# Batch 0 of a two-part attention and feed-forward kernel: pair 1's query copy on VectorE, sink rows loaded instead of copied, and another order of 390 pieces

## The chip, the cores and the metric

The kernel runs on one core of a Trainium2 chip. Its time is the device time in microseconds (us) of one execution; several runs are taken and their median is compared. Five engines work side by side, each through its own list of instructions in order: TensorE (PE in the profile, PEld for its weight loads), VectorE (DVE), ScalarE (ACT), GpSimd (POOL) and SyncE (SP), which here only issues loads and stores. Sixteen DMA engines move the data that SP, POOL and ACT ask for. PE writes to PSUM, a memory of eight banks, and the other engines bring results from there to SBUF. An instruction that needs another engine's result waits for a semaphore, and everything behind it on its engine waits with it.

## The reference

Attention over 4 batches, 8 heads, 768 tokens and 64 dimensions per head, and then a feed-forward layer with leaky slopes on all 3072 tokens:

```python
rel = pos[:, None] - pos[None, :]
causal = rel >= 0
stream_keep = causal & ((pos[None, :] < n_sink) | (rel < window))      # n_sink 4, window 64
mask = causal if is_retrieval[h] else stream_keep                       # heads 0, 2, 6 are retrieval heads
scores = where(mask, q @ k.T / sqrt(64), -1e9)
x = softmax(scores) @ v            # heads side by side: [3072, 512]
h = x @ w_in                       # [3072, 2048]
g = max(h, 0) + alpha * min(h, 0)
out = g @ w_out                    # [3072, 512]
```

A retrieval head sees all earlier tokens. A streaming head sees the last 64 tokens and the first four, the sink tokens.

## The kernel before

The heads of a batch are taken in four pairs, (2, 6), (1, 5), (0, 4), (3, 7). A pair of one batch has a number n from 0 to 15, so batch 0 has pairs 0 to 3. Pair 0 has two retrieval heads, pairs 1 and 3 two streaming heads, and pair 2 one of each (head 4 streams). The attention output of a batch becomes `xT`, and the feed-forward layer then works in token tiles t (512 and 256 tokens of each batch) and blocks f of 128 of the 2048 hidden features.

Every step is a small function with a name, and one list, `ORDER` (L14 to L81), says in which order the 1215 pieces are issued. Since each engine goes through its own instructions in that order, the list is the schedule of all engines at once. The names that matter here, with n the pair and hh the head within it:

- `Lq`, `Lk`, `Lv`: loads of queries, keys and values as 32-bit rows (SP's queue, L234 to L282); `Cq`, `Ck`, `Cv`: casts to bf16, in batch 0 mostly on POOL (L347 to L392).
- `Tq`, `Tk`: transposes of queries and keys by PE into a PSUM bank (L398); `tq`, `tk`: copies from there to SBUF (L408, L416). `tq` is on ACT but for `tq0.1`; `tk` is on VectorE in batch 0.
- `S`: scores on PE, into one of two double banks in batch 0; `s`: their exponential on ACT; `A`: scores times values on PE; `a`: the division on VectorE; `X`, `x`: transpose into `xT` on PE and its copy on VectorE.
- `wi`, `wo`: loads of the feed-forward weights, issued by POOL; `P`, `p`, `g`: first product, ReLU on ACT and slope on VectorE; `O`, `Q`: second product.
- `warm0` to `warm8`: 32, 3, 14 and then 4 each of dummy matmuls on PE (70 are used, `warm1` is not), and `kz`, `qz`, `vz`, `sz`, `so`, `ro`: fills.

In batch 0 a streaming head's keys are cut into seven tiles of 128 rows, four of which are the sink rows, repeated at the head of each tile. For the values, tile i holds rows 124 i to 124 i + 127, so its first four rows are at first ordinary rows of the sequence. `load_rows` (L261) loads tiles 0 to 5 of a head with one DMA of 128 partitions x 6 runs of 256 B (L277) and the short seventh tile with another one of 24 partitions (L282). The cast brings all to `vb`, and then `sinks` (L337) copies the four rows of tile 0 over the first four rows of tiles 1 to 6: on POOL for pairs 1 and 2 and head 3, on VectorE for head 7 (L387, L392).

On POOL the pieces of batch 0 come in this order: casts of keys and queries of pairs 1 to 3, the value cast `Cv0`, weights `wi1a wi0a wi1b wi0b`, `Cq3`, `Cv1`, `Cv2`, weights `wi6 wi7 wi5`, `Cv3.0`, `wi4`, `Cq4`, `Ck4.0`, `wi2`, `wi3`, `Ck4.1`, `Cq5`, and weights `wo`. On SP: `Lq0 Lk1 Lq1 Lk0 Lk2 Lq2 Lv0 Lk3 Lv1 Lq3 Lv2 Lv3 Lq4 Lk4 Lq5 Lk6 Lq6 Lk5` and on.

Of the kernel before, what the change touches and what calls it, by code (L numbers as in the profile page):

```python
# [17 lines left out]
Lk3 S0.1.0 kfz0 Lv1 vo ro0 Ck3.1 s0.1.0 Lq3 Ck3.0 wi1a wi0a wi1b wi0b Cq3 sz0 idf S1.0.0 so2 Al s1.0.0 so0 al S0.1.1  # L18
s0.1.1 Lv2 Tq2 Tk2 tk2.1 tk2.0 S0.1.2 S1.0.1 A0.0 s0.1.2 a0.0 Cv1 A0.1 a0.1 Cv2 s1.0.1 tq2 S1.1.1 Tk3 S2.0.1 tk3.0
s1.1.1 S2.0.2 X0 s2.0.1 x0 wi6 s2.0.2 wi7 Lv3 Lq4 Tq3 tk3.1 S2.0.0 wi5 m4.0.2 warm6 S2.1.0 A1.0 a1.0 Lk4 tq3 A1.1  # L20
Cv3.0 s2.0.0 Lq5 Lk6 Lq6 Lk5 wi4 Cq4 a1.1 S3.0.0 s2.1.0 A2.0 s3.0.0 X1 x1 S3.0.1 S3.1.1 Ck4.0 P0.2.0 s3.0.1 A3.0 a2.0
Lq7 a3.0 S2.1.1 s3.1.1 wi2 s2.1.1 Cv3.1 S3.1.0 wi3 A2.1 Ck4.1 Cq5 wo1 s3.1.0 P0.1.0 P0.3.0 A3.1 Lk7 P0.0.0 Tq4 a2.1
tq4 X2 a3.1 X3 Lv5 Tk4 x2 P0.2.1 Lv6 P0.1.1 tk4.0 P0.3.1 P0.0.1 x3 Tq5 tq5 tk4.1 P0.0.2 P0.1.2 wo0 p0.0 P0.3.2 P0.13
p0.13 g0.0 P0.14 g0.13 P1.14 wo3 p0.1 p1.14 g0.1 P1.2 p1.2 P0.8 Lv4 g1.14 Ck6.0 P0.9 g1.2 Cq6 m8.0.2 p0.8 nr p0.9 g0.8
m12.1.2 p0.3 near0 near2 P0.15 S4.0.5 p0.14 P1.10 s4.0.5 Ck6.1 P0.11 P0.2.2 g0.9 Ck5.1 g0.14 p0.15 p1.10 P1.0 Lq8 Tq6
ro1 Ck5.0 g0.15 p0.2 g0.3 S4.1.0 g1.10 wo2 p0.11 P1.12 P1.8 P0.7 g0.2 Lk8 s4.1.0 kfz1 g0.11 Lk9 p1.0 P0.5.0 p1.12 tq6
g1.0 P0.5.1 Tk5 P0.4.0 p1.8 P0.6 tk5.0 g1.8 p0.7 P0.4.1 g1.12 P0.5.2 P0.4.2 p0.6 tk5.1 P0.10 g0.7 p0.4 p0.10 g0.6
S4.0.3 s4.0.3 S4.0.0 P1.4 g0.4 Tk6 g0.10 S4.0.1 S5.1.0 m4.0.3 P1.6 p0.5 tk6.1 Ck7.0 near1 D1.0 P0.12 tk6.0 O0.0.0 g0.5
O0.0.1 p1.6 Lv7 p0.12 g1.6 p1.4 S6.1.1 D1.1 s5.1.0 s4.0.0 S5.1.1 S4.1.2 g1.4 m4.1.0 s4.0.1 s4.1.2 Z1.0.1 s6.1.1 s5.1.1
# [36 lines left out]
s14.0.4 m14.1.2 S14.0.1 b3.4.0 P5.0 a13.1 b4.4.0 p5.0 Q4.0.3 s14.0.1 Q4.0.7 g5.14 S15.1.2 g5.0 S14.1.1 S14.0.5 S15.0.0  # L66
m13.0.1 b5.4.0 m12.1.1 Z4.1.2 S14.0.0 b7.4.1 S15.1.1 m14.0.4 Q4.0.4 s15.1.2 Z4.1.4 s14.0.0 s14.1.1 s14.0.5 m14.0.0
m14.0.1 Cv14 m12.1.0 Q4.1.6 b6.4.0 s15.1.1 m14.0.5 A13.0 b2.4.1 m14.0.3 s15.0.0 S15.0.2 S15.1.0 S15.0.1 S14.1.0
s15.0.2 s14.1.0 m15.0.0 Q4.1.5 s15.1.0 m14.1.1 m14.1.0 A12.1 a13.0 A14.0 s15.0.1 m15.0.2 m15.1.1 a12.1 A14.1 a14.0
Q5.0.1 m15.1.0 a14.1 b3.4.1 b4.4.1 m15.0.1 Q4.1.7 m15.1.2 b1.5.0 X13 X12 b5.4.1 Q5.0.2 Q4.1.3 A15.0 Z5.0.1 X14 a15.0  # L70
A15.1 a15.1 Q4.1.4 b6.4.1 P6.8.0 X15 x15 P6.15.0 P6.4.0 b8.4.0 P6.8.1 P6.11.0 P6.10.0 b8.4.1 b7.5.0 P6.13.0 P6.4.1
# [5 lines left out]
Q6.0.6 b2.6.0 b1.6.1 P7.8 p7.12 Z6.1.3 Q6.0.5 p7.10 Q6.0.2 g7.10 Q6.1.2 g7.14 Z6.1.2 p7.8 g7.8 Q7.0.1 b3.6.0 b4.6.0
Q6.1.6 Z6.0.4 Q6.0.3 g7.12 b7.6.0 b8.6.0 b2.6.1 Q6.0.7 Z7.0.1 Z7.0.3 b3.6.1 b5.6.0 Q6.1.5 Q7.0.5 b4.6.1 Q6.0.4 Z6.1.4
b1.7.0 Z7.0.2 Q7.0.2 Q6.1.7 Q7.0.6 Q6.1.3 b5.6.1 b4.7.0 b2.7.0 b7.6.1 b7.7.0 b6.6.0 b8.6.1 b3.7.0 Q6.1.4 Q7.0.7 b6.6.1
Z7.0.4 Q7.0.3 b5.7.0 Q7.0.4 b8.7.0 b6.7.0  # L80
# [916 lines left out]
```

## Time and profile before

| | us |
|---|---|
| median of three runs | 222.54 (222.44 to 223.9) |
| span of the profiled execution, first to last instruction | 220.4 |
| PE busy in that span | 214.5 |
| VectorE busy | 188.0 |
| ACT busy | 145.8 |
| POOL busy | 45.6 |

The page gives the span of the profiled execution but no time of its own for it, so sums are made in the span, and what lies around it is the difference to the median, 2.1 us. A row of a timeline reads: start in us, duration in us, engine, source line of the kernel, operation, tile written <- tile read, shapes, count, and in brackets how long the engine was idle before and what ended that. A duration of several instructions in a row is one merged stretch. A "q" behind an engine is its queue of issues, so SPq L277 is SP issuing the DMA of line 277; how long that takes is not how long the data take. In a row of stretches stand the window, its length, the busy time of PE, PEld, VectorE, ACT and POOL with counts, the granted clock of PE, the share of time in which the 16 DMA engines were busy, and GB/s. In the part on DMA queues q1 holds the loads and stores that SP and ACT issue, q0 those of POOL: packets, MB and share of the 16 engines' span.

### The profile page before, as it was taken

How to read it: one execution, taken by the hardware profiler on the slowest of the kernel's cores; microseconds unless marked ns; L12 is line 12 of the kernel's file. 1: busy time of each engine (PE TensorE's matmuls, PEld its weight loads, DVE VectorE, ACT ScalarE, POOL GpSimd, SP SyncE). 2: the span in 40 equal slices, each digit the busy share in tenths (PEclk: the TensorE clock that was granted, in tenths of full speed). 3: DMA queues.
4: the chain of work that ended last, by engine and by line, in shares of the span. 5: the costliest groups of instructions: out<-in, count | busy, mean ns of one | idle time of the engine just before them, and what ended most of it. 6: DMA issues, size and time to landing. Idle time of an engine off the chain costs nothing.

```text
span 220.4 us, 5779 instructions
## 1 busy us (share of the span) xinstructions
PE 214.5 (97%) x2210; PEld 158.0 (72%) x2210; DVE 188.0 (85%) x471; ACT 145.8 (66%) x314; POOL 45.6 (21%) x92
## 2 busy tenths in 40 slices
PE   8989999999999999999999999999999999999993
PEld 7879866765465865577899666757889645888882
DVE  6879849979989897999998998999999767997841
ACT  4789659989999795657953165799783066816230
POOL 6679980620031200000004110100000200001000
PEclk9999999999999999999999999999999999999999
DMA  6999999999999999979999998791004310002124
GB/s 187 319 233 222 307 241 231 227 201 218 205 245 167 259 162 222 198 182 193 211 215 174 228 184 194 176 187 42 4 1 123 103 79 0 0 3 95 51 93 147
DMA packets 89655, 35.98 MB, mean 163 GB/s; under 512 B 76676, under 2 KB 87964, under 8 KB 89628
## 3 DMA queue, kind: packets, MB, share of 16 engines
q1 hardware_dynamic: 83484, 26.35, 59.4%
q0 software_dynamic: 5824, 8.93, 17.8%
q8 instruction: 17, 0.28, 0.5%
q10 hardware_dynamic: 320, 0.34, 0.5%
q14 instruction: 10, 0.08, 0.1%
HBM read 27.58 MB, written 6.29 MB: 154 GB/s over the span
## 4 chain that ended last, share of the span: by engine, by line
PE 92%; DVE 3%; ACT 2%; issue 1%
PE P L640 36%; PE P L718 28%; PE P L595 7%; PE P L660 7%; PE P L473 4%; PE P L814 3%; PE P L456 2%; PE P L406 2%; PE P L466 1%; PE P L620 1%; DVE kT L435 1%; PE P L544 1%; DVE g L652 1%; ACT neg L645 1%; ACT kT L435 0%
## 5 line engine op out<-in xcount | busy, mean ns | idle before, releaser
L640 PE MATMUL P<-xT,w_in_b 128*128 128x512 bf16 (+1 forms) x512 | 89.6, 326 | 0.0
L652 DVE SCALAR_TENSOR_TENSOR g<-neg,oma,P 128x256 bf16<-128x256 f32 (+1 forms) x128 | 71.7, 607 | 11.4 <-ACT neg L645 11.0
L645 ACT ACTIVATE neg<-P 128x512 f32<-128x512 f32 x96 | 55.4, 602 | 30.3 <-PE P L640 15.7
L640 PEld LDWEIGHTS <-w_in_b 128*128 128x128 bf16 x512 | 49.2, 98 | 29.1 <-issue 0.3
L718 PEld LDWEIGHTS <-g 128*128 128x128 bf16 x480 | 45.7, 98 | 8.1 <-issue 0.8
L512 ACT ACTIVATE eR<-P 128x448 bf16<-128x448 f32 (+4 forms) x63 | 37.0, 627 | 4.8 <-PE P L505 2.2
L718 PE MATMUL P<-w_out_b,g 128*128 128x256 bf16 x320 | 39.0, 273 | 0.0
L736 POOL DMA_DIRECT2D out_dram<-ot x14 | 7.6, 545 | 115.6 <-ACT ot L760 37.9
L560 ACT ACTIVATE eS<-P 128x352 bf16<-128x352 f32 x45 | 20.8, 494 | 2.3 <-PE P L473 1.4
L606 DVE TENSOR_TENSOR xn<-P,rcp 128x448 bf16<-128x448 f32 (+1 forms) x32 | 19.4, 607 | 1.1
L571 DVE TENSOR_TENSOR eS<-eS,ms_near 128x352 bf16<-128x352 bf16 x45 | 15.8, 363 | 0.7 <-ACT eS L560 0.6
L660 PE MATMUL P<-w_out_b,g 128*128 128x512 bf16 x64 | 15.8, 379 | 0.2 <-ACT kT L429 0.2
L703 DVE TENSOR_TENSOR g<-g 128x1024 bf16<-128x1024 bf16 x20 | 13.7, 683 | 0.1
L456 PE MATMUL P<-qT,kT 128*128 128x192 bf16 (+14 forms) x68 | 11.1, 251 | 0.2 <-ACT eS L566 0.2
L595 PEld LDWEIGHTS <-eS 128*128 128x128 bf16 x260 | 10.0, 97 | 1.3
L595 PE MATMUL P<-vb,eS 128*128 128x65 bf16 x260 | 10.8, 193 | 0.0
L522 DVE TENSOR_TENSOR eR<-eR,mr_near 128x128 bf16<-128x128 bf16 (+5 forms) x54 | 10.6, 223 | 0.0
L473 PE MATMUL P<-qT,kT 64*128 64x176 bf16 (+10 forms) x164 | 10.4, 249 | 0.0
L718 PE MATMUL P<-w,g 128*128 128x256 bf16 x80 | 10.4, 273 | 0.0
L660 PEld LDWEIGHTS <-g 128*128 128x128 bf16 x64 | 5.6, 97 | 6.3 <-issue 1.1
L595 PE MATMUL P<-vb,eR 128*128 128x65 bf16 x276 | 10.0, 193 | 0.0
L595 PEld LDWEIGHTS <-eR 128*128 128x128 bf16 x276 | 9.4, 97 | 0.6 <-issue 0.2
(130 smaller groups left out, 267.8 us busy)
## 6 DMA issues: line engine op xcount, KB each, us to landing
out_dram<-ot POOLq DMA_DIRECT2D x18, 256.0 KB, 3.2
rows<-in_k_dram SPq DMA_DIRECT2D x21, 192.0 KB
rows<-in_q_dram SPq DMA_DIRECT2D x18, 192.0 KB
rows<-in_v_dram SPq DMA_DIRECT2D x17, 192.0 KB
rows<-in_v_dram SPq DMA_DIRECT2D x14, 196.0 KB
rows<-in_q_dram SPq DMA_DIRECT2D x7, 384.0 KB
w_out_b<-in_moe_w_out_dram POOLq DMA_DIRECT2D x4, 512.0 KB, 15.1
rows<-in_k_dram SPq DMA_DIRECT2D x9, 196.0 KB
```

The lines of the kernel that those rows point to most:

```text
L456: nc.tensor.matmul(to, keys, queries, start=True, stop=stop)
L473: nc.tensor.matmul(to, keys[own], queries[own], start=True, stop=True)
L512: nc.scalar.activation(ebuf[n, hh][:, lo:hi].rearrange("p (x c) -> p x c", x=len(parts)), P[:, got[0]:got[0] + len(parts), 0:(hi - lo) // ...
L560: nc.scalar.activation(slots, sc[:, 0:352].rearrange("p (s c) -> p s c", c=176), AF.Exp, scale=scale)
L571: nc.vector.tensor_tensor(slots, slots, ms_near[:, 0:2, :] if m == 0 else ms_near[:, 1:3, :], op=ALU.mult)
L595: nc.tensor.matmul(pav[:, i, :], e[:, o:o + 128], vv[:, j, hh, 0:D + 1], start=(m == 0), stop=(m == len(terms) - 1))
L606: nc.vector.tensor_tensor(xn[n][:, 0:nt, D * hh:D * hh + D], pav[:, :, 0:D], rcp.to_broadcast([128, nt, D]), op=ALU.mult)
L640: nc.tensor.matmul(psg[:, w * i:w * (i + 1)], w_in_b[:, c, 128 * fb:128 * (fb + 1)], xT[:, c, o:o + w], start=(x == 0), stop=(x == 3))
L645: nc.scalar.activation(neg[t, f], bank(held["P", t, f][0]), AF.Relu, scale=-1.0)
L652: nc.vector.scalar_tensor_tensor(g_buf[t % 2][:, fb, 0:w], neg[t, f][:, c], oma[:, fb:fb + 1], bank(got[0])[:, c], op0=ALU.mult, op1=ALU.add)
L660: nc.tensor.matmul(bank(held["O", t, s][0]), g_buf[t % 2][:, f, 128 * s:128 * (s + 1)], w_out_b[:, f, :], start=(f == 0), stop=(f == 15))
L718: nc.tensor.matmul(q_bank(t, u, CHAIN[y]), left[t, u][y][:, f, :], right[y][:, f, :], start=(first and f == 0), stop=(f == 7), skip_group_ ...
```

## The change

Three things change.

1. `tq1`, the copy of pair 1's transposed queries from PSUM, goes from ACT to VectorE.
2. The five streaming heads of batch 0 get their sink rows from memory. The load of tiles 0 to 5 leaves out the first four partitions (124 partitions x 6 runs of 256 B), the load of the seventh tile too (20 partitions), and one more small DMA per head loads the four sink rows into all seven tiles (4 partitions x 7 runs of 256 B). `sinks` and its calls go.
3. Pieces 8 to 397 of `ORDER` stand in another order. The loads keep their order among themselves, and so do POOL's pieces. PE's, ACT's and VectorE's do not. PE's list before began `warm0 warm8 warm5 warm3 Tq0.0 Tk0.0 warm2 Tk1 S0.0.1 Tq0.1 S0.0.0 warm7 Tq1 S0.0.2 Tk0.1 S1.1.0 ...`.

```diff
-busy zero id warm0 kz3 Lq0.0 sz1 vz2 nms nmr so1 vz0 Lq0.1 Lk1 warm8 warm5 warm3 kz1 qz0 one Lq1 Lk0 La Ck0.0 kz2
-Cq0.0 Tq0.0 tq0.0 Tk0.0 qz warm2 Lk2 Lq2 kz0 tk0.0 Ck1.0 Ck1.1 Cq0.1 Tk1 S0.0.1 s0.0.1 Tq0.1 S0.0.0 Cq1 warm7 Lv0
-tk1.0 sz2 vz1 vz3 Tq1 Ck0.1 S0.0.2 s0.0.0 tk1.1 Tk0.1 Ck2.1 tq1 S1.1.0 s0.0.2 Ck2.0 warm4 tq0.1 s1.1.0 Cq2 tk0.1 Cv0
...
+busy zero id warm0 kz3 Lq0.0 sz1 vz2 kz0 Lq0.1 nms warm6 kz1 Lk1 nmr Lq1 Lk0 warm4 Ck0.0 Ck1.0 kz2 warm2 Cq0.0 sz2 Tk0.0
+La warm5 tk0.0 Tq0.0 Ck1.1 qz0 Lk2 qz Cq0.1 tq0.0 Cq1 Tk1 warm8 S0.0.0 Ck0.1 vz0 S0.0.1 Lq2 s0.0.0 Tq0.1 vz1 Ck2.1 tk1.0
+Ck2.0 Tq1 s0.0.1 S0.0.2 tk1.1 Cq2 Tk0.1 Lv0 s0.0.2 tq1 vo Cv0 Lk3 S1.1.0 S1.0.0 s1.1.0 Tq2 tq0.1 tk0.1 s1.0.0 warm3 Tk2
+sz0 S0.1.1 Lv1 S0.1.0 A0.0 kfz0 idf tq2 s0.1.1 S0.1.2 s0.1.0 Al vz3 tk2.0 s0.1.2 Ck3.1 Ck3.0 so1 so2 Tk3 wi1a a0.0
+S1.0.1 so0 wi0a tk2.1 A0.1 wi1b s1.0.1 S1.1.1 s1.1.1 S2.0.1 wi0b s2.0.1 Lq3 Cq3 warm7 S2.0.2 Tq3 S2.0.0 m12.1.2 s2.0.2
+Cv1 Lv2 Cv2 al tq3 tk3.0 A1.1 a0.1 S2.1.0 A1.0 s2.0.0 ro0 wi6 a1.1 Lv3 a1.0 X0 x0 wi7 s2.1.0 S3.0.0 Lq4 wi5 X1 tk3.1 x1
+S3.0.1 s3.0.0 Lk4 A2.0 a2.0 Cv3.0 S2.1.1 s3.0.1 S3.1.0 Cv3.1 P0.3.0 s2.1.1 A3.0 Lq5 s3.1.0 S3.1.1 a3.0 P0.2.0 A2.1 wi4
+Cq4 Ck4.0 a2.1 s3.1.1 A3.1 wi2 wi3 a3.1 P0.1.0 Ck4.1 Tq4 X2 P0.0.0 Cq5 x2 wo1 X3 x3 Lk6 Tk4 P0.3.1 tq4 P1.0 near0 P0.3.2
...
```
```diff
-            step = 128 if RETR[h] else 124
-            nc.sync.dma_start(dst[:, 0:6, hh, :], dram(src, o, [[D, 128], [step * D, 6], [1, D]]))
+            step, first = (128, 0) if RETR[h] else (124, NSINK)
+            nc.sync.dma_start(dst[first:128, 0:6, hh, :],
+                              dram(src, o + first * D, [[D, 128 - first], [step * D, 6], [1, D]]))
...
-            o = (n // 4 * H + heads(n)[hs[0]]) * S * D + 744 * D
-            nc.sync.dma_start(dst[0:24, 6, hs[0]:hs[-1] + 1, :], dram(src, o, [[D, 24], [apart, len(hs)], [1, D]]))
+            o = (n // 4 * H + heads(n)[hs[0]]) * S * D
+            both = slice(hs[0], hs[-1] + 1)
+            nc.sync.dma_start(dst[NSINK:24, 6, both, :], dram(src, o + 748 * D, [[D, 20], [apart, len(hs)], [1, D]]))
+            for hh in hs:
+                nc.sync.dma_start(dst[0:NSINK, :, hh, :],
+                                  dram(src, (n // 4 * H + heads(n)[hh]) * S * D, [[D, NSINK], [0, NT], [1, D]]))
...
-    def sinks(n, rows, of=range(2), copy=nc.gpsimd.tensor_copy):
-
-        for hh in of if n < LAY else ():
-            if not RETR[heads(n)[hh]]:
-                vh = rows[0:NSINK, hh, :, 0:D].bitcast(fp32)
-                copy(vh[:, 1:7, :], vh[:, 0:1, :].to_broadcast([NSINK, 6, D // 2]))
-
...
-        sinks(n, vv.rearrange("p t h c -> p h t c"), [hh], (nc.gpsimd.tensor_copy, nc.vector.tensor_copy)[hh])
...
-        sinks(n, vv.rearrange("p t h c -> p h t c"))
...
-                item(f"tq{n}", put_q, ("q", n), n, slice(0, 128), "A")
+                item(f"tq{n}", put_q, ("q", n), n, slice(0, 128), "V" if n == 1 else "A")
```

More of the change, by code (lines that the diff above doesn't have):

```diff
@@ L20 @@
[L20 to L29, printed above, removed]
@@ new lines @@
+S3.0.1 s3.0.0 Lk4 A2.0 a2.0 Cv3.0 S2.1.1 s3.0.1 S3.1.0 Cv3.1 P0.3.0 s2.1.1 A3.0 Lq5 s3.1.0 S3.1.1 a3.0 P0.2.0 A2.1 wi4
+Cq4 Ck4.0 a2.1 s3.1.1 A3.1 wi2 wi3 a3.1 P0.1.0 Ck4.1 Tq4 X2 P0.0.0 Cq5 x2 wo1 X3 x3 Lk6 Tk4 P0.3.1 tq4 P1.0 near0 P0.3.2
+P0.14 tk4.0 P0.2.1 tk4.1 p1.0 wo0 P0.1.1 P0.2.2 p0.3 one P0.0.1 P1.2 Tq5 g1.0 p0.14 wo3 g0.14 p0.2 g0.3 tq5 S4.0.1 p1.2
+Lq6 nr P1.14 g0.2 P0.0.2 p0.0 Lk5 s4.0.1 g1.2 P0.10 p0.10 g0.0 S4.0.3 p1.14 m4.0.2 P0.8 Cq6 Ck6.1 g1.14 Ck6.0 p0.8 P1.10
+g0.8 P1.8 near2 P0.1.2 ro1 p0.1 p1.8 P0.6 g0.10 S4.1.0 Ck5.1 s4.0.3 p1.10 P0.5.0 g1.8 p0.6 P0.9 Ck5.0 s4.1.0 P0.12
@@ L67 @@
 m13.0.1 b5.4.0 m12.1.1 Z4.1.2 S14.0.0 b7.4.1 S15.1.1 m14.0.4 Q4.0.4 s15.1.2 Z4.1.4 s14.0.0 s14.1.1 s14.0.5 m14.0.0
[L68 to L71, printed above, removed]
@@ L77 @@
[L77 to L80, printed above, removed]
+m14.0.1 Cv14 m12.1.0 Q4.1.6 b6.4.0 s15.1.1 m14.0.5 A13.0 b2.4.1 m14.0.3 s15.0.0 S15.0.2 S15.1.0 S15.0.1 S14.1.0 s15.0.2
@@ L81 @@
+Q7.0.2 Q6.1.7 Q7.0.6 Q6.1.3 b5.6.1 b4.7.0 b2.7.0 b7.6.1 b7.7.0 b6.6.0 b8.6.1 b3.7.0 Q6.1.4 Q7.0.7 b6.6.1 Z7.0.4 Q7.0.3
+b5.7.0 Q7.0.4 b8.7.0 b6.7.0
 """.split()
```

78 lines of the change are left out of this document (42 added, 36 removed).

## The prediction

> **What bounds the kernel now.** I read the page first, then stretches, then the first 30 us engine by engine. The page:
>
> ```profile
> span 220.4 us, 5779 instructions
> PE 214.5 (97%) x2210; PEld 158.0 (72%) x2210; DVE 188.0 (85%) x471; ACT 145.8 (66%) x314; POOL 45.6 (21%) x92
> ...
> q1 hardware_dynamic: 83484, 26.35, 59.4%
> q0 software_dynamic: 5824, 8.93, 17.8%
> ...
> PE 92%; DVE 3%; ACT 2%; issue 1%
> ```
>
> TensorE (PE) is 97% of the span and 92% of the chain that ended last. Work that PE loses early comes back nowhere. So the question for every edit is whether PE waits longer or shorter. The places where it waits before 31 us:
>
> ```profile
> 10.49 0.49 PE L406 MATMUL P<-ident,g 128*128 128x128 bf16 x6 [0.39 <-DVE kT L437]
> ...
> 12.54 0.24 PE L456 MATMUL P<-qT,kT 128*128 128x192 bf16 x1 [0.16 <-ACT eS L566]
> ...
> 13.76 0.23 PE L778 MATMUL P<-ident_f,alpha_r 16*128 16x16 f32 x1 [0.40 <-DVE ident_f L324]
> ```
>
> That is 0.39 + 0.16 + 0.40 = 0.95 us: all that a better order of the first 30 us can win there. What it can lose is bounded by the loads. The DMA engines by stretch (last two columns: their busy share, where over 1 means overlapping packets, and GB/s):
>
> ```profile
> 14.00:24.00 10.00, 10.00 (x196) 9.31 (x197) 7.76 (x21) 8.35 (x12) 9.08 (x16) 1.00 1.13 244
> 24.00:34.00 10.00, 10.00 (x125) 7.19 (x123) 5.91 (x14) 6.39 (x11) 8.41 (x13) 1.00 1.16 260
> ...
> 57.00:62.00 5.00, 5.00 (x44) 2.43 (x39) 4.38 (x11) 4.90 (x13) 1.86 (x3) 1.00 1.00 206
> ```
>
> From 14 us on the 16 DMA engines have no free time. Batch 0's values are loaded in the middle of that, and PE uses them almost as they land:
>
> ```profile
> 10.64 1.80 SPq L277 DMA_DIRECT2D rows<-in_v_dram  x2
> 13.38 0.38 SPq L240 DMA_DIRECT2D rows<-in_q_dram  x1
> 15.46 1.61 SPq L277 DMA_DIRECT2D rows<-in_v_dram  x2
> ...
> 17.75 0.87 POOL L351 CAST g<-rows 128x768 bf16<-128x768 f32 x1
> ...
> 23.72 0.56 POOL L386 CAST vb<-rows 128x448 bf16<-128x448 f32 x1 [0.45 <-DVE xn L606]
> 24.34 0.34 POOL L342 COPY vb<-vb 4x192 f32<-4x192 f32 x1
> 24.63 0.61 POOL L824 DMA_DIRECT2D w_in_b<-in_moe_w_in_dram  x1
> ```
> ```profile
> 24.90 0.56 PE L595 MATMUL P<-vb,eS 128*128 128x65 bf16 x13
> ```
>
> Lv3, pair 3's values, is issued at 15.46. Cv3.0, its cast on GpSimd (POOL), starts at 23.72, the sink copy ends at 24.68, and A3.0 on PE starts at 24.90: a slack of 0.2 us. The cast's row blames a VectorE operation that had long been done. SyncE's own waits in 14 to 30 us say what it was:
>
> ```profile
> SPq L254 <- DMA rows<-in_v_dram: 1.6, 1, 1.6
> SPq L240 <- DMA rows<-in_v_dram: 1.2, 1, 1.2
> ```
>
> SyncE's next loads waited for those same value loads. The second, Lq6, goes out at 23.81. So Lv3 landed at about 23.7.
>
> **The load's new shape.** Five value loads of batch 0 (heads 1, 5, 4, 3, 7) change from 128 rows of 6 x 256 B to 124 rows. The bytes hardly change. What matters is how a DMA is dealt out to the 16 engines. No view prints it, but the trace keeps each DMA's completion signals. On the first of the eight semaphores that SyncE's loads use there are 284 signals for 20 DMAs. That comes out exactly if a load of 128, 112 or 96 rows and a transpose signal 16 times, the 24-row tail 13 times, and each of three 4-row sink loads 5 times: 16 x 16 + 13 + 3 x 5 = 284. So 24 rows go to 12 engines (not 16) and one signal covers the absent four; 4 rows go to 4. The count is the largest divisor of the rows that is at most 16. The divisors of 124 are 1, 2, 4, 31, 62, 124: it would go to **4 engines**. The Trainium skill's page "DMA: Bandwidth & Descriptors", section "Why a DMA increments its semaphore by 16 and not by 1", states that rule (largest k up to 16 that divides the dims, on the lowest-numbered engines) and speaks against the change; the 13 and 5 signals agree, and no run yet shows 124 rows.
>
> Price: 128 rows x 6 runs on 16 engines are 48 runs each; 124 x 6 on 4 engines are 186. If it is the same four each time (if not: rival 3), those get 5 x (186 - 48) = 690 runs more over the five loads. One run of 256 B costs, from the 57 to 62 us row, where nearly all loads are of such runs: 16 engines x 256 B / 206 GB/s = 20 ns. Low end, from the densest row here, where runs are longer:
>
> ```profile
> 8.00:10.00 2.00, 2.00 (x31) 1.72 (x29) 1.97 (x7) 1.89 (x3) 1.39 (x3) 1.00 1.14 347
> ```
>
> 16 x 256 B / 347 GB/s = 12 ns. High end, q1's mean: 0.594 x 16 x 220.4 us / 83484 = 25 ns. I take 20, as it is the same kind of run: 690 x 20 ns = **13.8 us** (8.1 to 17.3). Later loads are spread over all 16 engines and so wait for the slowest four.
>
> **Part by part, in PE time.**
>
> - *Lv1 (2 loads).* Lq3, pair 3's queries, is queued behind it on SyncE, and comes 2 x 138 x 20 ns = 5.5 us later. Cq3, the cast at 17.75, moves to some 23, and Tq3 on PE and then A1 (Cv1 is behind Cq3 on POOL) wait. This is contained in the next, as the later wait ends last.
> - *Lv3.* Lands at 23.7 + 13.8 + 0.7 (five sink loads, 7 runs on each of 4 engines: 35 x 20 ns) = 38.2. Cv3.0 takes 0.56: 38.8. A3.0 goes from 24.90 to 38.8, 13.9 later. The new order has S2.1.1, S3.1.0 and P0.3.0 ahead of A3.0 in place of S3.1.1 and P0.2.0. S2.1.1 is like S3.1.1 and P0.3.0 like P0.2.0; S3.1.0 is more, eight matmuls of this kind:
>
> ```profile
> 25.64 0.24 PE L456 MATMUL P<-qT,kT 128*128 128x192 bf16 x1
> ...
> 26.22 0.25 PE L544 MATMUL P<-nms,ident 128*128 128x192 bf16 x1
> ```
>
> Seven steps take 26.22 - 25.64, so eight take 0.66 us. Left: 13.9 - 0.66 = **13.2 us** of PE waiting.
> - *Queued behind Cv3.0 on POOL:* wi4, Cq4, Ck4, wi2, wi3, Cq5, wo. They move by the same 14 us, and PE's users of them (Tq4, P0.8 to P0.11) also do, so they cost no more. The weights wi6, wi7, wi5 go out later, while Lv3 is still served, and take their turn on the four engines: 3 loads x 256 runs / 16 x (0.178 x 16 x 220.4 / 5824 = 108 ns) = 5.2 us. Part of that lay before 23.7 already; I leave it for the top of the range.
> - *Sink copies out.* Four on POOL, 0.34 us each (row at 24.34), and one on VectorE. POOL saves 1.4 us; as Cv3.0 waits for its load this is worth nothing.
> - *Sink loads in.* Five more issues on SyncE, before Lq3, Lv3, Lq4 and all that follows:
>
> ```profile
> L273 SPq DMA_DIRECT2D rows<-in_v_dram x15: 328/450/3941, 36.0 to 136.3; - x15
> ```
>
> 5 x 0.45 = 2.3 us of issue, hidden by the loads already queued at a share above 1; if that cover were gone, 2.3 us.
> - *tq1 to VectorE.* It leaves ACT and enters VectorE between tk1.1 and tq0.1:
>
> ```profile
> 9.75 0.79 ACT L411 COPY qT<-P 128x768 bf16<-128x768 bf16 x1
> ...
> 10.25 0.19 DVE L437 COPY kT<-P 64x28 bf16<-64x28 bf16 x1
> 10.35 0.96 DVE L411 COPY qT<-P 64x768 bf16<-64x768 bf16 x1
> ...
> 10.82 0.25 PE L456 MATMUL P<-qT,kT 128*128 128x192 bf16 x1
> ```
>
> ACT saves 0.8. VectorE pays about 0.96 (on 128 partitions not shown; between 0.79 and twice 0.96). Before, tq1 ended at 10.54; now it starts when tk1.1 ends (10.44, the 10.25 row) and ends at 11.4, so S1.1.0, which was at 10.82, waits 0.6 us. Behind it on VectorE are vo, tq0.1, tk0.1, which S0.1 needs.
> - *Warm-up.* Ahead of the first transposes there are now 32 + 4 + 4 + 14 = 54 dummy matmuls, not 44. The total stays 70.
>
> ```profile
> 1.06 3.17 PE L814 MATMUL P<-busy 128*128 128x128 bf16 x28 [1.06 <-DVE zero L324]
> ...
> 6.12 0.79 ACT L411 COPY qT<-P 64x768 bf16<-64x768 bf16 x1
> 6.35 0.96 PE L814 MATMUL P<-busy 128*128 128x128 bf16 x14
> ...
> 7.48 0.54 PE L456 MATMUL P<-qT,kT 128*128 128x448 bf16 x3
> ```
>
> Fourteen take 0.74 us from first to last start (0.96 less about 0.22 for the last), 57 ns each, so ten more are 0.57 us; Tq0.0 now follows Tk0.0 and four more of them (0.57 + 0.34 + 0.23, where six transposes count as six such matmuls), so tq0.0 ends near 6.91 + 1.1 = 8.0, and S0.0 starts there instead of at 7.48. Four of the matmuls taken out of the later stretch (0.23) are won back: PE loses some 0.3.
> - *The other order.* It can fill at most the 0.95 us; I credit half. Net of the small parts: 0.3 + 0.6 - 0.5 = **+0.4 us**, which lies ahead of A3.0 and is covered by its wait.
> - *Clock.* The first 28 matmuls took 113 ns each, later ones 57. If a wait of 10 us brought that back for some 4 us, it would cost up to 2 us; no wait in this trace is that long, so I take 0 to 2. The Trainium skill's "TensorE: Matmul & The Clock Gate", Part 1, says that an idle window of about 3.4 us brings half clock back; by it the sum would be nearer the upper value.
>
> Sum: 13.2, with 0 to 2 for the clock on top, and less what a run may be cheaper than 20 ns while twelve engines rest. For these two together I take 0.7 off: **+12.5**. The profiled span of 220.4 becomes 232.9; the median, 222.54, lies 2.1 above that span (dispatch and end, unchanged), so **235**.
>
> **Rivals.**
>
> 1. *The 124-row loads are spread evenly* (chance 0.06). For it: no such load is in the trace. Against: the 24-row signals. Then only the small parts count: +0.4, 222.9, with 1 either way.
> 2. *Spread evenly, and the order wins* (0.02). POOL is rid of its copies, ACT of tq1, and PE's three waits of 0.95 us close: 221.6, not slower. It decides if S1.1.0 finds tq1 done, that is if PE has work until 11.4. Against it: PE's order there holds only Tk0.1 between S0.0.2 and S1.1.0.
> 3. *Four engines, but a cheaper price* (0.22): each load takes another four, or a run takes 12 ns when few engines work. At 12 ns Lv3 lands at 32.3, A3.0 follows at 32.8: 7.9 - 0.6 = +7.3, 229.8. With different fours Lv1's and Lv3's two loads overlap and about half of 8.1 us is left: +4, 226.5.
> 4. *Four engines, and weights and clock on top* (0.20): 13.2 + 5.2 + 2 = +20.4, 243; half of the weights, 240.
>
> **Numbers.** The forecast has the remaining 0.50: 231 to 239. Likeliest time 235. The range 227 to 242 leaves out rivals 1 and 2 and the outer edges of 3 and 4. About 1% (2.2 us) is what one can tell from no change here. Faster by that: 0.01 (rival 2 gives only 0.4%). Within: 0.07 (1 and 2). Slower: 0.92.
>
> **What would show it.** On four engines: a DMA share well under 0.7 between 18 and 38 us, since twelve engines have little to do; POOL's casts of pair 3's queries and of values 1, 2, 3 idle before them on a DMA; a PE wait of several us ahead of A3.0, near 38 us, and earlier ones at Tq3 and A2.0; after it the same PE work at the same pace. If instead the share stays above 1 and Cv3.0 starts before 26 us, the loads were spread and rival 1 holds. If tq1's row on VectorE is above 1.2 us, its price was too low. The forecast is wrong, too, if the waits appear but sum to under 6 us.

## The result: 5% slower, and the profile after

The changed kernel takes 234.52 us (median of 6 runs, 232.15 to 235.59) against 222.51 us for the kernel before (6 runs, 222.13 to 223.9): a ratio of 1.0518, with a 95% interval of 1.0475 to 1.056. The forecast was 235.0, in a range of 227 to 242. The profiled execution took 233.78 us, of which its span is 231.7, so 2.1 us lie around it, as before.

The page of the changed kernel, whose rows stand beside those of the page before:

```profile
span 231.7 us, 5790 instructions
...
PE 218.9 (94%) x2210; PEld 161.5 (70%) x2210; DVE 188.5 (81%) x471; ACT 145.0 (63%) x313; POOL 44.7 (19%) x88
...
PEclk9999597999999999999999999999999999999999
DMA  6949399999999999999899899886101530002114
...
q1 hardware_dynamic: 83438, 26.35, 56.3%
...
PE 85%; DMA 7%; issue 3%; POOL 2%; SPq 1%; ACT 0%; DVE 0%; POOLq 0%
```

The loads move the same 26.35 MB in nearly the same number of packets. But DMA, which was not among the leaders of the chain, now has 7% of it. The span is 11.3 us longer, and two rows say in what form: PE's idle time (span less busy) went from 220.4 - 214.5 = 5.9 us to 231.7 - 218.9 = 12.8, that is 6.9 more, and PE's busy time rose by 4.4 us though it executes the same 2210 matmuls. The slices of 5.8 us show why it is busy longer: the granted clock falls to 5 in the fifth slice and 7 in the seventh.

Where PE idles, from the waits of PE in 5 to 60 us (what waited, for what, us in total, times, longest):

```profile
PE P L401 <- POOL g L348: 4.9, 1, 4.9
PE P L590 <- POOL vb L383: 2.7, 1, 2.7
PE P L451 <- DVE qT L406: 0.5, 1, 0.5
```

The first is Tq3, which waits for Cq3; the second A3.0, which waits for Cv3.0; the third S1.1.0, which waits for pair 1's queries on VectorE. Before, the longest wait there was 0.40 us. When they end, from PE's timeline:

```profile
25.16 0.82 PE L401 MATMUL P<-ident,g 128*128 128x128 bf16 x6 [4.92 <-POOL g L348]
...
36.45 0.82 PE L590 MATMUL P<-vb,eS 128*128 128x65 bf16 x13 [2.67 <-POOL vb L383]
```

Both casts, `Cq3` and `Cv3.0`, waited in their turn for loads. Their rows, and GpSimd's waits in the same stretch:

```profile
24.28 0.83 POOL L348 CAST g<-rows 128x768 bf16<-128x768 f32 x1 [5.87 <-DMA rows<-in_q_dram]
...
35.83 0.56 POOL L383 CAST vb<-rows 128x448 bf16<-128x448 f32 x1 [6.16 <-DMA rows<-in_v_dram]
```

```profile
POOL vb L383 <- DMA rows<-in_v_dram: 6.2, 1, 6.2
POOL g L348 <- DMA rows<-in_q_dram: 6.1, 2, 5.9
```

The stretches (columns as before: after ACT and POOL come granted clock, DMA share and GB/s) of the kernel after show DMA engines that are partly idle ahead of each of PE's two waits:

```profile
12.00:16.00 4.00, 3.71 (x54) 3.30 (x55) 3.45 (x10) 2.89 (x4) 2.11 (x5) 1.00 0.47 102
...
20.00:24.00 4.00, 0.24 (x4) 0.05 (x1) 0.57 (x2) 1.22 (x2) 0.00 (x0) 0.86 0.95 205
24.00:28.00 4.00, 2.84 (x28) 2.48 (x29) 0.26 (x2) 1.73 (x2) 2.76 (x4) 0.50 0.34 74
28.00:32.00 4.00, 4.00 (x67) 3.85 (x66) 2.81 (x6) 1.97 (x3) 1.67 (x3) 0.79 0.79 111
...
36.00:40.00 4.00, 3.55 (x48) 2.97 (x48) 1.60 (x5) 0.49 (x1) 2.53 (x5) 0.57 1.10 315
```

In the kernel before, the first and the third of these were

```profile
12.00:16.00 4.00, 3.44 (x47) 2.82 (x46) 2.54 (x9) 3.27 (x5) 2.76 (x5) 1.00 0.95 224
...
24.00:28.00 4.00, 4.00 (x72) 3.29 (x70) 3.65 (x9) 2.17 (x4) 3.94 (x8) 1.00 1.15 294
```

So between 12 and 16 us, and again between 24 and 28, 102 and 74 GB/s are moved where 224 and 294 were. The clock row also gives the size of the busier PE: from 25.16 to 28 half of the time is lost (1.4 us), from 28 to 32 a fifth (0.8), and from 36 to 40 0.43 of 3.55 us (1.5), 3.7 us of the 4.4.

Last, SyncE's queue (start, us, line). Lq4 is the row of L239 at 30.92:

```profile
10.40 3.43 SPq L276 DMA_DIRECT2D rows<-in_v_dram  x2
13.94 2.53 SPq L283 DMA_DIRECT2D rows<-in_v_dram  x1
...
18.65 5.91 SPq L283 DMA_DIRECT2D rows<-in_v_dram  x1
...
24.95 2.59 SPq L276 DMA_DIRECT2D rows<-in_v_dram  x2
...
30.92 0.39 SPq L239 DMA_DIRECT2D rows<-in_q_dram  x1
```

Issues that take 0.3 to 0.5 us each are held for up to 5.9 us, so the queue was not free to give the idle engines work. The loads' completion signals, which the trace keeps though no view prints them, say more about these holds. Between 10 and 31 us five issues took over 2 us (two of them are the second issues of the rows at 10.40 and 24.95). Each stood directly behind a 124-row load, and each ended 1.9 to 2.3 us before that load had landed: the issue at 13.94 ends at 16.47, and pair 1's second value load lands at 18.36; the one at 18.65 ends at 24.56, and pair 2's lands at 26.54. SyncE's loads signal on eight semaphores in turn, but these did not hold the five: the semaphore of each had had its last signal 1.4 to 8.0 us before the hold began. A limit on the runs that wait at a DMA engine would fit, but no run varies that alone.

### The profile page after: what moved, and what is told of

It is laid out like the page before. It is cut to its first block, busy times and chain, and to the rows that moved or that the text cites. A ratio compares the mean times of both kernels' runs of the same rounds, so it can differ in the third digit from the quotient of the medians.

```text
span 231.7 us, 5790 instructions
## 1 busy us (share of the span) xinstructions
PE 218.9 (94%) x2210; PEld 161.5 (70%) x2210; DVE 188.5 (81%) x471; ACT 145.0 (63%) x313; POOL 44.7 (19%) x88
## 3 DMA queue, kind: packets, MB, share of 16 engines
q1 hardware_dynamic: 83438, 26.35, 56.3%
## 4 chain that ended last, share of the span: by engine, by line
PE 85%; DMA 7%; issue 3%; POOL 2%; SPq 1%; ACT 0%; DVE 0%; POOLq 0%
PE P L635 36%; PE P L713 27%; PE P L590 7%; PE P L655 6%; PE P L468 4%; DMA rows<-in_k_dram 3%; DMA rows<-in_v_dram 2%; DMA rows<-in_q_dram 2%; PE P L401 2%; PE P L461 1%; POOL w_in_b L814 1%; SPq L253 1%; PE P L451 1%; PE P L615 1%; PE P L539 0%
## 5 line engine op out<-in xcount | busy, mean ns | idle before, releaser
L635 PE MATMUL P<-xT,w_in_b 128*128 128x256 bf16 (+1 forms) x512 | 90.8, 327 | 0.0
L713 PEld LDWEIGHTS <-g 128*128 128x128 bf16 x480 | 45.7, 98 | 8.1 <-issue 0.8
L600 DVE RECIPROCAL rcp<-P 128x7 f32<-128x7 f32 (+1 forms) x32 | 6.3, 195 | 11.0 <-PE P L590 10.9
L590 PE MATMUL P<-vb,eS 128*128 128x65 bf16 x260 | 12.4, 205 | 2.7 <-POOL vb L383 2.7
L590 PEld LDWEIGHTS <-eS 128*128 128x128 bf16 x260 | 11.6, 106 | 4.5 <-issue 3.5
L566 DVE TENSOR_TENSOR eS<-eS,ms_near 128x352 bf16<-128x352 bf16 x45 | 14.3, 333 | 0.3 <-ACT eS L555 0.3
L451 PE MATMUL P<-qT,kT 128*128 128x192 bf16 (+13 forms) x68 | 12.3, 269 | 0.7 <-DVE qT L406 0.5
L561 ACT ACTIVATE eS<-P 128x768 bf16<-128x768 f32 (+1 forms) x10 | 6.4, 650 | 8.3 <-PE P L539 8.2
L406 ACT COPY qT<-P 128x768 bf16<-128x768 bf16 (+1 forms) x7 | 5.6, 803 | 9.1 <-PE P L401 7.6
L468 PE MATMUL P<-qT,kT 64*128 64x176 bf16 (+12 forms) x167 | 10.9, 250 | 0.0
```

What stands on the lines that cost most here:

```text
L451: nc.tensor.matmul(to, keys, queries, start=True, stop=stop)
L468: nc.tensor.matmul(to, keys[own], queries[own], start=True, stop=True)
L566: nc.vector.tensor_tensor(slots, slots, ms_near[:, 0:2, :] if m == 0 else ms_near[:, 1:3, :], op=ALU.mult)
L590: nc.tensor.matmul(pav[:, i, :], e[:, o:o + 128], vv[:, j, hh, 0:D + 1], start=(m == 0), stop=(m == len(terms) - 1))
L635: nc.tensor.matmul(psg[:, w * i:w * (i + 1)], w_in_b[:, c, 128 * fb:128 * (fb + 1)], xT[:, c, o:o + w], start=(x == 0), stop=(x == 3))
L713: nc.tensor.matmul(q_bank(t, u, CHAIN[y]), left[t, u][y][:, f, :], right[y][:, f, :], start=(first and f == 0), stop=(f == 7), skip_group_ ...
```

## The experiments

Two theories were to be told apart. The *engine theory*, that of the prediction: a load of 124 rows is dealt to four DMA engines and everything else follows. The *small-load theory*: the additional small loads on SyncE's queue are what costs. Order and query copy were the third suspect. Each ratio is to runs of the kernel before beside them (222.51 us for the first row, 222.76 to 223.06 for the others).

| kernel | median us | ratio to before (95%) |
|---|---|---|
| changed kernel, 124 rows | 234.52 | 1.0518 (1.0475 to 1.056) |
| same, second time | 232.92 | 1.0463 (1.0424 to 1.0503) |
| changed loads alone | 234.39 | 1.0495 (1.0452 to 1.0537) |
| order and query copy alone | 223.13 | 1.0005 (0.9981 to 1.0029) |
| before, cut 124 + 4 | 235.43 | 1.0567 (1.0515 to 1.062) |
| before, cut 112 + 16 | 223.87 | 1.0038 (1.001 to 1.0066) |
| changed, cut 112 + 12 | 228.16 | 1.0207 (1.0163 to 1.0251) |
| changed, cut 62 + 62 (one run) | 249.26 | |
| order and query copy, cut 112 + 16, sinks copied | 223.53 | 1.0063 (1.003 to 1.0096) |
| changed loads cut 112 + 12, order of before | 229.47 | 1.0304 (1.0269 to 1.034) |
| changed, cut 112 + 12, small loads on GpSimd | 237.02 | 1.061 (1.0567 to 1.0652) |
| changed, waits filled (84, 44) | 233.42 | 1.0469 (1.0432 to 1.0507) |
| changed, waits filled (84, 100) | 233.54 | 1.0502 (1.0464 to 1.0541) |

### Which of the three parts

The changed kernel with the `ORDER` of before and `tq1` back on ScalarE, so that of the change only the loads are left:

```diff
-busy zero id warm0 kz3 Lq0.0 sz1 vz2 kz0 Lq0.1 nms warm6 kz1 Lk1 nmr Lq1 Lk0 warm4 Ck0.0 Ck1.0 kz2 warm2 Cq0.0 sz2 Tk0.0
+busy zero id warm0 kz3 Lq0.0 sz1 vz2 nms nmr so1 vz0 Lq0.1 Lk1 warm8 warm5 warm3 kz1 qz0 one Lq1 Lk0 La Ck0.0 kz2
...
-                item(f"tq{n}", put_q, ("q", n), n, slice(0, 128), "V" if n == 1 else "A")
+                item(f"tq{n}", put_q, ("q", n), n, slice(0, 128), "A")
```

> The kernel before, with its order and tq1 on ACT, and only the loads of the changed kernel: 124-row loads and small sink loads in place of the sink copies. Theory E: the loads alone do it, so 232 to 237 us with PE waiting at Tq3 and A3.0. Theory O: near 222.5. Theory S: also 232 to 237; the run before tells E and S apart.

Measured: 234.39 us, the whole loss. PE's waits are the two of the changed kernel:

```profile
PE P L402 <- POOL g L349: 5.7, 1, 5.7
PE P L591 <- POOL vb L384: 2.8, 1, 2.8
```

The converse, the kernel before with the new `ORDER` and `tq1` on VectorE, its loads and sink copies kept:

```diff
-                item(f"tq{n}", put_q, ("q", n), n, slice(0, 128), "A")
+                item(f"tq{n}", put_q, ("q", n), n, slice(0, 128), "V" if n == 1 else "A")
```

> The kernel before with the new order and tq1 on VectorE, but the old loads and sink copies. Theory E: what is left is the small parts, predicted as +0.4 us: 222.5 to 223.5. Theory O: near 234.5. If the new order closes PE's three early waits of 0.95 us: 221.6.

Measured: 223.13 us, a ratio of 1.0005 with an interval that holds 1. PE's waits there:

```profile
PE P L455 <- DVE qT L410: 0.5, 1, 0.5
PE P L594 <- POOL vb L341: 0.5, 1, 0.5
```

So the order and the query copy neither win nor lose what can be measured; the loads do it all.

### How many engines

The changed kernel with each 124-row load cut into two of 62 rows:

```diff
-            nc.sync.dma_start(dst[first:128, 0:6, hh, :],
-                              dram(src, o + first * D, [[D, 128 - first], [step * D, 6], [1, D]]))
+            for lo, hi in (((0, 128),) if first == 0 else ((4, 66), (66, 128))):
+                nc.sync.dma_start(dst[lo:hi, 0:6, hh, :],
+                                  dram(src, o + lo * D, [[D, hi - lo], [step * D, 6], [1, D]]))
```

> The changed kernel with each 124-row load cut into two loads of 62 rows. Theory E with the same lowest engines each time: 62 rows go to 2 engines, 186 runs each, both loads on the same two: 5 x (372 - 48) = 1620 runs more than before on them, at 14 ns (the changed kernel's Lv1.1 landed 2.6 us after Lv1.0, 186 runs) 22.7 us; values of pair 3 near 46 us and 242 to 247 us in all. Theory E with other engines for each DMA: about as the changed kernel, 234. Theory that only an odd start partition or a row count not a multiple of 16 as such costs, not the divisor: also about 234.

Measured: 249.26 us, in a single run. The completion signals show two engines for each such load, where a load of 124 rows shows four. The waits of PE are those of the changed kernel, grown:

```profile
PE P L591 <- POOL vb L384: 11.8, 1, 11.8
PE P L402 <- POOL g L349: 10.3, 1, 10.3
```

The sizes go together: two engines get 2 x 62 x 6 / 2 = 372 runs per head instead of 48, 1620 more over five heads, and the loss is 249.26 - 223.05 = 26.2 us; four engines get 690 more, and the loss is 12.0. The ratios are 2.3 and 2.2.

The same cut at another place, into 112 and 12 rows, spreads the loads over sixteen and twelve engines:

```diff
-            for lo, hi in (((0, 128),) if first == 0 else ((4, 66), (66, 128))):
+            for lo, hi in (((0, 128),) if first == 0 else ((4, 116), (116, 128))):
```

> The changed kernel, with each 124-row load of a streaming head cut into two loads, of 112 and of 12 rows, five DMAs more. Theory E (a load runs on as many engines as the largest divisor of its rows up to 16, so 124 rows on 4): 16 and 12 engines, the waits before Tq3 (4.9 us) and A3.0 (2.7 us) go, and so does the slow clock; 222.5 to 224 us. Theory S (the price is in the number of DMAs on SyncE, its issue and its completion semaphores): ten DMAs more than before, so no better than 234.5. Theory O (the new order or tq1 on VectorE): still near 234.5.

Measured: 228.16 us. More than half of the loss is gone, and so are the waits at Tq3 and A3.0 for pair 3. But 5 us are left, which the engine theory had not foreseen. PE now waits elsewhere, for the keys of pair 4 and for other values:

```profile
PE P L402 <- POOL natk L362: 3.3, 1, 3.3
PE P L591 <- POOL vb L388: 1.2, 1, 1.2
```

This version adds ten small loads to SyncE's queue, against the kernel before, where the changed kernel adds five. To hold the number of loads fixed and change the engines alone, the kernel before was cut in two ways. Everything else in it stays, the sink copies too:

```diff
-            nc.sync.dma_start(dst[:, 0:6, hh, :], dram(src, o, [[D, 128], [step * D, 6], [1, D]]))
+            for lo, hi in ((0, 128),) if RETR[h] else ((0, 124), (124, 128)):
+                nc.sync.dma_start(dst[lo:hi, 0:6, hh, :],
+                                  dram(src, o + lo * D, [[D, hi - lo], [step * D, 6], [1, D]]))
```

> The kernel before, with its order, its sink copies and its first 0-row starts; only each of its five 128-row loads of a sliding-window head is cut into rows 0 to 123 and rows 124 to 127. All values still arrive. Engine theory (a 124-row load is put on four DMA engines, whatever the kernel around it): 230 to 235 us, nearly the whole loss of the changed kernel, with TensorE waits of 2 us or more ahead of the transposes of pair 3's queries and of A3.0, and five completion signals per 124-row load. Rival (what costs is the number of small loads on SyncE's queue, each of which takes one of eight completion semaphores): the same time as the kernel cut into 112 and 16 rows, which has just as many loads, 224 to 227 us for both.

and

```diff
-            for lo, hi in ((0, 128),) if RETR[h] else ((0, 124), (124, 128)):
+            for lo, hi in ((0, 128),) if RETR[h] else ((0, 112), (112, 128)):
```

> As the kernel cut into 124 and 4 rows, but cut into 112 and 16 rows, so that both pieces divide by 16 and every load can spread over sixteen DMA engines. Engine theory: 222.5 to 224 us, the time of the kernel before within 0.5%. Small-load theory: five more loads on SyncE's queue cost about half of what the ten more loads of the 112 and 12 row version still lost (5 us), so 224.5 to 227 us, with casts that wait for DMAs although the sixteen engines have room.

Measured: 235.43 and 223.87 us. Two kernels with the same order, the same number of loads and the same bytes differ by 11.6 us by where each load is cut. PE's waits with 124 + 4 rows:

```profile
PE P L408 <- POOL g L353: 4.8, 1, 4.8
PE P L597 <- POOL vb L388: 3.7, 1, 3.7
```

With 112 + 16 rows the longest is

```profile
PE P L597 <- POOL vb L388: 0.9, 1, 0.9
```

and the stretch from 24 to 28 us in the one and in the other (DMA share and GB/s at the end):

```profile
24.00:28.00 4.00, 3.87 (x34) 3.46 (x35) 0.00 (x0) 2.06 (x3) 3.20 (x7) 0.50 0.30 67
```
```profile
24.00:28.00 4.00, 2.94 (x53) 2.45 (x51) 2.37 (x6) 1.63 (x4) 2.75 (x6) 1.00 1.18 271
```

The engine theory holds for the loss of the changed kernel. Five more loads by themselves cost 0.4% (0.1 to 0.7).

### What the 112 + 12 version still lost

Two runs take its parts apart. The first is the kernel cut into 112 and 16 rows with the changed order and query copy; it copies the sink rows as before, so against the 112 + 12 version the five 4-row sink loads are gone:

```diff
-            step, first = (128, 0) if RETR[h] else (124, NSINK)
-            for lo, hi in (((0, 128),) if first == 0 else ((4, 116), (116, 128))):
+            step = 128 if RETR[h] else 124
+            for lo, hi in ((0, 128),) if RETR[h] else ((0, 112), (112, 128)):
...
-            for hh in hs:
-                nc.sync.dma_start(dst[0:NSINK, :, hh, :],
-                                  dram(src, (n // 4 * H + heads(n)[hh]) * S * D, [[D, NSINK], [0, NT], [1, D]]))
...
+        sinks(n, vv.rearrange("p t h c -> p h t c"))
```

> The kernel before with the changed kernel's order and pair 1's queries copied by VectorE, sink rows still copied, and each of the five sliding-window loads cut into 112 and 16 rows: against the 112 and 12 row version of the changed kernel (228.2 us) only the five 4-row sink loads are gone. If those sink loads are what kept 5 us there, 223 to 225 us; if the later places of the loads in the new order leave no room for small loads, whichever they are, 226 to 229 us.

Measured: 223.53 us. The second is the version with the changed loads alone, cut likewise. It keeps all ten small loads and issues everything in the order of before:

```diff
-            nc.sync.dma_start(dst[first:128, 0:6, hh, :],
-                              dram(src, o + first * D, [[D, 128 - first], [step * D, 6], [1, D]]))
+            for lo, hi in (((0, 128),) if first == 0 else ((4, 116), (116, 128))):
+                nc.sync.dma_start(dst[lo:hi, 0:6, hh, :],
+                                  dram(src, o + lo * D, [[D, hi - lo], [step * D, 6], [1, D]]))
```

> The changed kernel's loads, cut into 112 and 12 rows, with its five sink loads, in the order of the kernel before and with pair 1's queries copied by ScalarE: ten more loads than before, as in the 112 and 12 row version of the changed kernel (228.2 us), but each issued at its old place, Lq3 5.5 us earlier. If ten more loads cost the 5 us whatever the order, 226.5 to 229 us; if only the new order has no room for them, 223 to 225 us.

Measured: 229.47 us. So the 4.6 us between 228.16 and 223.53 (4.3 if each is taken against the runs of the kernel before beside it) go with the five sink loads, and in the order of before it is 5.6, between 229.47 and 223.87. (The small pieces also have 12 rows in one version and 16 in the other, and the loads of the seventh tile 20 and 24.) SyncE's queue shows where: with the sink loads, pair 4's queries (L239) go out at 24.57, after a tail load that was held

```profile
17.87 4.04 SPq L277 DMA_DIRECT2D rows<-in_v_dram  x4
23.47 0.28 SPq L284 DMA_DIRECT2D rows<-in_v_dram  x1
...
24.57 0.39 SPq L239 DMA_DIRECT2D rows<-in_q_dram  x1
```

and without them at 20.78:

```profile
17.14 2.77 SPq L277 DMA_DIRECT2D rows<-in_v_dram  x4
20.01 0.34 SPq L283 DMA_DIRECT2D rows<-in_v_dram  x1
20.78 0.38 SPq L239 DMA_DIRECT2D rows<-in_q_dram  x1
```

In the version with them the waits of SyncE's own queue have, in 8 to 40 us,

```profile
SPq L284 <- DMA rows<-in_v_dram: 1.5, 1, 1.5
```

A tail load, that of a seventh tile, could not be issued until an earlier value load had landed. The completion signals say why: of the eight semaphores, the tail's had belonged to the 112-row load issued eight loads earlier, whose last signal came at 23.41, and the tail went out at 23.47; the sink load behind it went out at 23.88, its own semaphore having had its last signal at 23.86. A small load takes one of the eight as a large one does. Ahead of this wait the last issue of the row at 17.87 had been held for 2.53 us with its semaphore free, so here both kinds of hold follow one another.

The small loads were then taken off SyncE:

```diff
-                nc.sync.dma_start(dst[lo:hi, 0:6, hh, :],
+                (nc.gpsimd if hi - lo == 12 else nc.sync).dma_start(dst[lo:hi, 0:6, hh, :],
...
-                nc.sync.dma_start(dst[0:NSINK, :, hh, :],
+                nc.gpsimd.dma_start(dst[0:NSINK, :, hh, :],
```

> The 112 and 12 row version of the changed kernel (228.2 us), with its ten small loads (five of 12 rows, five of 4 sink rows) issued on GpSimd's queue instead of SyncE's. If the 5 us that it still lost come from SyncE's eight completion semaphores, which ten small loads take from the large ones, it is at 222.5 to 225 us. If they come from the small loads themselves on the DMA engines (short pieces, whichever queue issues them), it stays at 227 to 229 us. If GpSimd's time of issue counts (ten issues between casts that already end the waits), the casts of pair 3 and 4 come later by some us and it is at 228 to 233 us.

Measured: 237.02 us, worse than the changed kernel. The large loads do go out now: between 12 and 16 us the DMA share is 1.19,

```profile
12.00:16.00 4.00, 3.33 (x42) 2.92 (x43) 3.43 (x9) 2.81 (x5) 3.58 (x7) 1.00 1.19 236
```

where it was 0.70 with all loads on SyncE:

```profile
12.00:16.00 4.00, 3.81 (x64) 3.35 (x62) 3.38 (x11) 3.57 (x5) 2.00 (x5) 1.00 0.70 128
```

But GpSimd issues the small loads in its own order, behind its casts:

```profile
22.76 0.64 POOL L277 DMA_DIRECT2D rows<-in_v_dram  x1
...
29.15 0.93 POOL L388 CAST vb<-rows 128x896 bf16<-128x896 f32 x1 [5.14 <-DMA rows<-in_v_dram]
...
30.67 1.15 POOL L277 DMA_DIRECT2D rows<-in_v_dram  x2
...
39.10 0.56 POOL L384 CAST vb<-rows 128x448 bf16<-128x448 f32 x1 [4.78 <-issue]
```

Pair 2's value cast waits 5.14 us for its load, part of which GpSimd had issued at 22.76; pair 3's small loads stand behind that cast and go out at 30.67 only; and Cv3.0 starts at 39.10. The third case of the expectation came, by more than was expected (228 to 233). The run says that SyncE's queue had kept the DMA engines idle between 12 and 16 us. It cannot say what the small loads would cost on a queue without work in front of them.

### The clock

The changed kernel with matmuls on a constant tile in PE's two waits:

```diff
-    for i, n in enumerate((32, 3, 14, 4, 4, 4, 4, 4, 4)):
+    for i, n in enumerate((32, 3, 14, 4, 4, 4, 4, 4, 4, 84, 44)):
...
-S1.0.1 so0 wi0a tk2.1 A0.1 wi1b s1.0.1 S1.1.1 s1.1.1 S2.0.1 wi0b s2.0.1 Lq3 Cq3 warm7 S2.0.2 Tq3 S2.0.0 m12.1.2 s2.0.2
+S1.0.1 so0 wi0a tk2.1 A0.1 wi1b s1.0.1 S1.1.1 s1.1.1 S2.0.1 wi0b s2.0.1 Lq3 Cq3 warm7 S2.0.2 warm9 Tq3 S2.0.0 m12.1.2 s2.0.2
...
-S3.0.1 s3.0.0 Lk4 A2.0 a2.0 Cv3.0 S2.1.1 s3.0.1 S3.1.0 Cv3.1 P0.3.0 s2.1.1 A3.0 Lq5 s3.1.0 S3.1.1 a3.0 P0.2.0 A2.1 wi4
+S3.0.1 s3.0.0 Lk4 A2.0 a2.0 Cv3.0 S2.1.1 s3.0.1 S3.1.0 Cv3.1 P0.3.0 s2.1.1 warm10 A3.0 Lq5 s3.1.0 S3.1.1 a3.0 P0.2.0 A2.1 wi4
```

> The changed kernel, with 84 matmuls on a constant tile into scratch put ahead of the transposes of pair 3's queries, and 44 ahead of A3.0, where TensorE now waits 4.9 and 2.7 us; the values are not changed. The two slow stretches after those waits (granted clock 0.50 to 0.57) are the question. If they lie on the path, keeping the array busy gives back the part of the second that nothing later hides, 1.5 to 2.5 us: 232 to 233 us. If the casts that end the waits would come no earlier and the slow work between the two waits is hidden by the second wait, as it should be for the first stretch, only the second counts, 1 to 1.7 us: 232.8 to 233.5. If the clock is no matter: 234.5 to 235.5, since the filling matmuls may run a little past the end of the wait.

Measured: 233.42 us. The second filling had ended 3.4 us before its cast did, and a slow stretch still followed. So it was made 100 long (44 becomes 100 in the first line of the diff), beside a second measurement of the changed kernel:

> The changed kernel with matmuls on a constant tile in both waits, 84 ahead of the transposes of pair 3's queries as in the filled version (233.4 us) and 100 instead of 44 ahead of A3.0, since there the 44 were done 3.4 us before the cast, and a slow stretch of 4 us (granted clock 0.61 and 0.54) still followed. If the slow stretches are a term of their own, about 1.7 us more come back: 231.3 to 232.6 us, 1.5 to 3 us below the changed kernel. If the clock is no matter, 233.4 to 235 us.

> The changed kernel once more, as the measure beside which the filled one is read: 233.5 to 235.5 us.

Measured: 233.54 us filled, 232.92 unfilled; their intervals overlap. The stretch from 36 to 40 us in the filled kernel, in the changed kernel's second profile (two rows) and in its first (above, clock 0.57):

```profile
36.00:40.00 4.00, 3.48 (x67) 2.85 (x66) 2.27 (x7) 0.49 (x1) 2.69 (x5) 1.00 1.07 358
```
```profile
36.00:38.00 2.00, 1.68 (x34) 1.35 (x34) 1.14 (x4) 0.49 (x1) 1.10 (x2) 1.00 1.06 368
38.00:40.00 2.00, 1.88 (x29) 1.51 (x30) 1.67 (x6) 0.57 (x1) 2.00 (x5) 1.00 1.10 344
```

In the second profile PE's wait ahead of A3.0 was shorter, and no slow stretch came after it:

```profile
PE P L401 <- POOL g L348: 4.6, 1, 4.6
PE P L590 <- POOL vb L383: 1.6, 1, 1.6
```

Its span is 230.1 us against 231.7. With the clock at full speed throughout, the filled kernel (span 231.1) is no faster than that: Cv3.0 is set by loads and started at 36.09 there, and PE, done sooner, has to stay for it. The slow stretch after the first wait costs nothing of its own, as the second wait takes it up. The one after the second wait costs about 1 us, in those executions in which it comes: from the start of A3.0 to the end the span had 195.2 us left with it (231.7 - 36.45), 194.1 without it (230.1 - 35.96) and 194.4 filled (231.1 - 36.70). The clock row gave 1.5 us of busy time for it. Medians don't resolve it.

## Why the prediction was right, step by step

- *PE bounds the kernel, and lost time comes back nowhere.* Right: after A3.0 no wait of PE above 0.2 us is listed before 60 us, and the median keeps 12.0 us.
- *124 rows go to four engines, the same four each time.* Right. Each of the five loads signals four times as its parts land. The pair 124 + 4 and 112 + 16 shows it by time (235.43 and 223.87), two engines by size (249.26). The rule of the Trainium skill's "DMA: Bandwidth & Descriptors", section "Why a DMA increments its semaphore by 16 and not by 1", the largest count up to 16 that divides the rows, agrees with all three: 4, 16 and 2 engines.
- *A run costs 20 ns.* Too dear: pair 1's two loads, which follow each other on the four engines, landed at 15.76 and 18.36 us, 2.6 us for 186 runs, 14 ns. By that, 690 runs are 9.7 us, not 13.8.
- *Lv3 lands at 38.2, A3.0 starts at 38.8, 13.2 us of PE waiting.* Cv3.0 started at 35.83 and A3.0 at 36.45, so 36.45 - 24.90 - 0.66 = 10.9 us. At 14 ns a run, service alone (690 runs, and 35 more for the sink loads) would give 23.7 + 9.7 + 0.5 = 33.9. For the other 1.9 us there are two candidates that the step left out. SyncE's queue was held behind the slow loads, so Lv3, issued at 15.46 before, was issued from 24.95 on. And GpSimd's weight loads came in between: the signals show that pair 3's 124-row loads had landed at 29.47 and 32.44, but the load of its seventh tiles only at 35.29 and head 3's sink load at 35.69, 0.14 us before the cast; between 32.5 and 33.5 us all 209 packets that moved were of GpSimd's queue. How the 1.9 us divide was not measured. The misses in this term have opposite signs. Which limit held the queue stays open; the eight semaphores it was not.
- *Lq3 is late, Cq3 moves to some 23, contained in the later wait.* Cq3 started at 24.28, and Tq3's wait of 4.9 us made the later one shorter (2.7). The sum is right, not the picture of a wait of several us at A2.0 too: none is listed there.
- *Weights and casts behind Cv3.0 move along at no further cost.* For the casts this holds, as no later wait is listed. The weights' 5.2 us, left to the top of the range, can have come only in part: 1.9 us are all that the trace leaves for them and the held queue together, and no run separates the two.
- *Sink copies out are worth nothing.* Right: with the copies kept, the 112 + 16 versions stand at 223.53 and 223.87.
- *Sink loads: 5 x 0.45 = 2.3 us of issue, hidden by the loads already queued at a share above 1.* This step fails as a statement about the sink loads. Where the other loads are spread well, they go with 4.6 us, twice the issue time, since what they take is SyncE's place and one of its eight semaphores, and not only its time. The share was not above 1 at that time: it fell to 0.47 between 12 and 16. How much of the changed kernel's own 12 us is theirs was not measured; no run keeps its 124-row loads and leaves out every further small load.
- *tq1 on VectorE takes 0.96, and S1.1.0 waits 0.6; the warm-up costs 0.3 and the order wins 0.5; together +0.4 and covered.* The wait was 0.50, and the copy took what was assumed for it:

```profile
11.10 0.96 DVE L406 COPY qT<-P 128x768 bf16<-128x768 bf16 x1
```

Order and copy alone measure +0.1 us, less than the interval.
- *Clock 0 to 2 us.* The profiled execution has about 1 us of it on the path. The Trainium skill's "TensorE: Matmul & The Clock Gate", Part 1, puts an idle window of about 3.4 us ahead of half clock; here a wait of 2.67 us was enough in one execution, and one of 1.56 us in another was not.
- *The sum.* +12.5 was forecast, +12.0 came: 10.9 at A3.0 and about 1 of slow clock make 11.9, against 11.3 in the span. That it fits so closely is partly luck: a price of a run that was too high stood for a held queue and for weights that came in between, neither of which was in the sum.
- *What would show it.* "A DMA share well under 0.7 between 18 and 38 us" was wrong as put: it is 0.86 over that stretch. It is low in spells only: 0.47 between 12 and 16 us, ahead of that stretch, and 0.34 between 24 and 28, but 0.95 between 20 and 24.

Of the rivals, the even spread (222.9) fell with the two cuts, and with it the order that wins. The cheaper price (226.5 to 229.8) was nearer in the price of a run and missed the held queue. The last one (240 to 243) had the clock right in kind but at twice its size, and with the whole of the weights on top it is too slow.

## What to carry to other kernels

A load's row count decides how many DMA engines work on it, so before rows are trimmed from a transfer, look at the divisors: four rows fewer made 16 engines into 4 here, and the same rows cut as 112 + 16 cost under 1%. Look for it in the profile as a low DMA share and GB/s ahead of a wait for that load, and in the number of completion signals. Count small loads as places in an in-order queue, not as bytes or issue time, and before moving them to another engine's queue see what stands in front of them there.

## What had not been expected of the hardware

- SyncE's issue of a small load was held 2.53 us from 13.94 on, in a stretch in which the DMA engines were busy 0.47 of the time, and 5.91 us from 18.65 on, after which 74 GB/s were moved.
- Five loads of 4 rows x 7 runs of 256 B (35 KB in all) went with 4.6 us.
- The granted clock fell to half after a wait of 2.67 us in the records, and full speed in its place gave nothing that the medians show.
